# Attention beside a gated feed-forward gate: down-projection transposed, six output row buffers, a reciprocal placed later, and ScalarE in the end stage

## The chip, the core and the metric

The kernel runs on one core of one Trainium2 chip. A core has TensorE (PE in the profile; PEld is its weight load), VectorE (DVE), ScalarE (ACT), GpSimd (POOL) and SyncE (SP), which here issues nearly all the DMAs. The metric is the device time of one execution in microseconds.

## What is computed

x is 2048 tokens x 640 features, in bf16. The result is x + s * g.

```
xn  = layernorm(x)
qkv = xn @ wqkv                      # 32 heads of 20
s   = (softmax(q k^T / sqrt(20)) v) @ wo
h   = sigmoid(xn @ w_gate) * (xn @ w_up)      # 1728 wide
g   = silu(h @ w_down)
out = x + s * g
```

## The kernel before

Tokens are cut into four chunks of 512 (`QC`), and the heads into eight groups of four (`GH`). A group and a chunk make a block, so there are 32 blocks (`NBLK`), numbered in the order in which they are worked. A block has 64 score tiles: 128 keys by 512 queries of one head.

**The start** normalizes x and writes it transposed to `xnT` (features on the partitions). **The main stage** is one loop from L1240 on. It is a planner that runs when the program is built: it advances a clock `now` in steps of 0.02 us, keeps the time at which each engine is free and each PSUM bank is released, and issues the next instruction of each engine when its own durations (`T_F`, `T_MM`, ...) say that it can run. What it fixes is the order of the instructions on each engine; the waits are semaphores.

The work that it interleaves:

- Score tiles (`score_mm`, L899) and their exponentials. A tile goes to ScalarE (`exp_act`: `pt` for two tiles in the two-bank tiles `scA`, `px` for one in a flexible bank) or to VectorE (`iv`, L1336, then three passes over four tiles, L1030 to L1036, giving `pb`). Whichever engine is free takes the next tile.
- The products with v (`pv_emit`, L937) into one bank, `oacc`.
- The items: k, q and v projections, the gate and up products (`mk_gu`, L665), the down-projection (`mk_down`, L720) and the output projection (`mk_out`, L774). An item takes one of three flexible PSUM banks (`bank`), runs its matmuls in steps between the others' work, and then its ScalarE and VectorE operations; the last of these frees the bank. Matmuls of items are cut in four groups of 32 columns that run side by side (`cols`, L472).

Constants steer the choices: `LEAD` is how far the feed-forward items may run ahead of their due work, `M_ORD` the order of banks tried for an item, `DORD` the order for a score tile of VectorE and `XORD` that for the extra tile of ScalarE.

**Gate.** sigmoid is built from tanh. For each chunk 14 tiles `hT` (features of h on the partitions, 512 tokens) are made. `mk_down` then takes, for each of four token tiles of 128 and two halves of 320 output features, hT as the stationary operand and `wd` as the moving one: 14 steps of four matmuls over 320 columns. Tanh on ScalarE (`td`) and one VectorE pass give the gate with tokens on the partitions, in fp32 (`gqs`). For chunks 0 to 2 it is stored in DRAM (`gq_dram`, L743); for the last chunk it stays in two SBUF buffers (`gq_last`, L714).

**Normalization of a block.** After the last product, `norm_a` (L967) copies `oacc` to `on` on VectorE, and SP sends the row sums to DRAM (`ld`, L972) and back spread over 128 partitions (`lt`, L974). `norm_b` (L977) takes the reciprocal on VectorE (`rt`), sends it out (`rd`, L982) and loads it broadcast (`rl`, four DMAs, L985). GpSimd multiplies (`on_bf`), and `norm_c` moves the result to `oU` by DMAs. The planner puts `norm_b` a fixed time behind the copy: 9.0 us (`T_LT`) for blocks up to 27, and 4.5 us (`T_L2`) for blocks 28 to 30 (L1288).

**Output.** For chunks 0 to 2, `mk_out` projects a token tile in two halves of 320 features, once its block is normalized. `load_out` (L765) brings x and the gate of a tile into one of three buffers in the dead `xnT`, one tile ahead, with no tile loaded ahead across a chunk's end. VectorE multiplies with the gate (L796), GpSimd or, from tile 8 on (`DVE_ADD`), VectorE adds x, and SP stores.

**The end stage** (`chain`, L1135) follows the last product of block 31: copy, transposes and division, then the last part of the output projection into four banks of 512 features (`mains`) and two of the narrow rest (`rest`). VectorE multiplies each wide bank with the gate (`t_main`) and the narrow ones (`t_rest`); GpSimd adds x for the first two tiles, VectorE for the last two; SP and ScalarE's queue store two tiles each (`t_out`).

SP works its queue in order: a DMA that waits holds back all that stand behind it.

Of the kernel before, what the change touches and what calls it, by code (L numbers as in the profile page):

```python
# [52 lines left out]
def kernel(  # L53
# [40 lines left out]

    gq_dram = dram.tile([S, D], FP32, name="gq_dram", tag="gqd", bufs=1)
    NU = (HEADS - PG * GH) // UH
# [350 lines left out]
    T_IV, T_ON = 0.605, 0.60  # L447
    LATE, T_LT, T_OU, T_L2, T_RL = 1.0, 9.0, 1.5, 4.5, 5.6
    T_PASS = (0.1333, 0.1333, 0.27)
# [19 lines left out]
    def mark(*e):  # L469
        return lambda t: ev_at.__setitem__(e, t)  # L470
# [194 lines left out]
    def mk_gu(c, kf, at):  # L665
# [20 lines left out]
        def th():  # L686
            st["t"] = w2.tile([P, QC], BF16, tag="tnh", bufs=2, name="tnh")
            act_imm(st["t"][0:fs, :], st["g"][0:fs, :], ACT.Tanh, 0.5)
# [8 lines left out]
        def th2():  # L697
            st["t"] = w2.tile([P, QC], BF16, tag="tnh", bufs=2, name="tnh")
            act_imm(st["t"][fs:P, :], st["g"][0:fs, :], ACT.Tanh, 0.5)
# [13 lines left out]

    def gq_last(t4):  # L714
        if len(gq_l) == t4 // 2:
            w = w2.tile([P, 2, KD, 2 * P], BF16, tag="wgu", bufs=2, name="gql")
            gq_l.append(w.rearrange("p i k f -> p (i k f)").bitcast(FP32))
        return gq_l[t4 // 2][:, t4 % 2 * D:(t4 % 2 + 1) * D]

    def mk_down(c, t4, h, at):  # L720
        st = {}
        tt = 4 * c + t4

        def alloc():
            st["ps"] = misc_ps()

        def mm(kf):
            cols(st["ps"][:, 0:HD], hT[:, kf, t4 * P:(t4 + 1) * P], wd[:, kf, h * HD:(h + 1) * HD],
                 kf == 0, kf == NFT - 1)

        def th():
            st["td"] = w2.tile([P, HD], BF16, tag="td", bufs=2, name="td")
            act_imm(st["td"], st["ps"][:, 0:HD], ACT.Tanh, 0.25)

        def ev():
            if c == NQC - 1:
                return nc.vector.scalar_tensor_tensor(out=gq_last(t4)[:, h * HD:(h + 1) * HD], in0=st["td"], scalar=1.0,
                                                      in1=st["ps"][:, 0:HD], op0=ALU.add, op1=ALU.mult)
# [6 lines left out]
        return Item([("PE", alloc, [(0.14, lambda kf=kf: mm(kf)) for kf in range(NFT)]),  # L745
                     ("ACT", 0.32, th), ("DVE", 0.40, ev, "free", mark("d", c, t4, h))], at, pre=[("h", c, kf) for kf in range(NFT)])

# [8 lines left out]
    def div_scale(tps, n):  # L756
# [6 lines left out]
        return onq  # L763

    def load_out(tt):  # L765
# [4 lines left out]
        out_tiles[tt] = (o2[:, 0:D], o2[:, D:3 * D].bitcast(FP32))  # L770
        nc.sync.dma_start(out=out_tiles[tt][0], in_=x2[tt * P:(tt + 1) * P, :])
        nc.sync.dma_start(out=out_tiles[tt][1], in_=gq_dram[tt * P:(tt + 1) * P, :])

    def mk_out(tt, h, at):  # L774
        st = {}

        def alloc():
            if h == 0:
                load_out(tt)
                if (tt + 1) % 4:  # L780
                    load_out(tt + 1)
            st["ps"] = misc_ps()
# [5 lines left out]
        def ev():  # L788
            xr, gqr = out_tiles[tt]
            sl = slice(h * HD, (h + 1) * HD)  # L790
            while sum(x[1] == "o" for x in pool_q) > 2:
                x = next(x for x in pool_q if x[1] == "o")
                pool_q.remove(x)
                x[2]()
            tmp = w2.tile([P, 2 * HD], BF16, tag="gqs", bufs=3, name="otmp")[:, 0:HD]
            ins = nc.vector.scalar_tensor_tensor(out=tmp, in0=st["ps"][:, 0:HD], scalar=0.25,  # L796
                                                 in1=gqr[:, sl], op0=ALU.mult, op1=ALU.mult)

            if tt >= DVE_ADD:
                st["tmp"] = tmp  # L800
                return ins

            def part(i):
                cs = slice(h * HD + i * HD // 2, h * HD + (i + 1) * HD // 2)
                add = nc.gpsimd.tensor_tensor(out=xr[:, cs], in0=tmp[:, i * HD // 2:(i + 1) * HD // 2], in1=xr[:, cs], op=ALU.add)
                if h == 1 and i == 1:
                    nc.sync.dma_start(out=out2[tt * P:(tt + 1) * P, :], in_=xr)
                return add
            for i in range(2):
                pool_q.append((now + 0.6, "o", lambda i=i: part(i)))  # L810
            return ins
        def add():
            xr = out_tiles[tt][0][:, h * HD:(h + 1) * HD]
            ins = nc.vector.tensor_tensor(out=xr, in0=st["tmp"], in1=xr, op=ALU.add)
            if h == 1:
# [3 lines left out]
                     ("DVE", 0.40, ev, "free", mark("o", tt, h))] + ([("DVE", 0.24, add)] if tt >= DVE_ADD else []), at, need=ALT + 1 + 2 * (tt // 4),  # L819
                    pre=[("d", tt // 4, t4, i) for t4 in range(4) for i in range(2)] + [("h", 2, kf) for kf in range(NFT)] + (  # L820
                        [("o", tt - 2, 1)] if h == 0 and tt > 1 else []))
# [3 lines left out]
    for c in range(NQC):  # L825
        for kf in range(NFT):
            glu.append(lambda at, c=c, kf=kf: mk_gu(c, kf, at))
        for h in range(2):
            for t4 in range(4):
                glu.append(lambda at, c=c, t4=t4, h=h: [mk_down(c, t4, h, at)])  # L830
    for t in range(4 * NVP):
# [272 lines left out]
    xg = xl.rearrange("p (t u) -> p t u", u=D)  # L1104

    def t_main(t4):
        nc.vector.scalar_tensor_tensor(out=tmps[t4], in0=mains[t4], scalar=0.25, in1=gq_last(t4)[:, 0:512],
                                       op0=ALU.mult, op1=ALU.mult)
        if t4 < 2:
            nc.gpsimd.tensor_tensor(out=tail[t4][:, 0:512], in0=tmps[t4], in1=tail[t4][:, 0:512], op=ALU.add)  # L1110

    def t_rest(i):
        nc.vector.scalar_tensor_tensor(out=tmp[:, 2 * i:2 * i + 2, :],
                                       in0=rest[i][:, 0:2 * EX].rearrange("p (t e) -> p t e", e=EX),
                                       scalar=0.25, in1=gq_l[i].rearrange("p (t u) -> p t u", u=D)[:, :, 512:D],
                                       op0=ALU.mult, op1=ALU.mult)
        (nc.vector if i else nc.gpsimd).tensor_tensor(out=xg[:, 2 * i:2 * i + 2, 512:D], in0=tmp[:, 2 * i:2 * i + 2, :],
                                                      in1=xg[:, 2 * i:2 * i + 2, 512:D], op=ALU.add)

    def t_last(t4):  # L1120
        nc.vector.tensor_tensor(out=tail[t4][:, 0:512], in0=tmps[t4], in1=tail[t4][:, 0:512], op=ALU.add)

# [4 lines left out]

    def t_done(i):
        t_rest(i)
        for t4 in (2 * i, 2 * i + 1):  # L1130
            if i:
                t_last(t4)
            t_out(t4)
# [7 lines left out]
             ("DVE", 0.63, lambda: t_main(0), (10,)), ("DVE", 0.63, lambda: t_main(1), (10,)),  # L1141
             ("DVE", 0.7, lambda: t_done(0), (10,)),
             ("PE", 1.1, lambda: e_late(1), (9,), (0, 1, 2, 3)),
             ("DVE", 0.63, lambda: t_main(2), (14,)), ("DVE", 0.63, lambda: t_main(3), (14,)),
             ("DVE", 1.3, lambda: t_done(1), (14,))]
    chain_end = {}

# [21 lines left out]
    with tc.manual_schedule(engines={ENG.PE, ENG.Activation, ENG.DVE, ENG.Pool}):  # L1169
# [70 lines left out]
        while len(chain_end) < len(chain) or fill or items or glu_items or any(it.i < len(it.ops) for it in active):  # L1240
# [37 lines left out]
            for eng in ("ACT", "DVE"):  # L1278
# [260 lines left out]
```

## Time and profile before

| | us |
|---|---|
| median of 3 runs | 802.56 (802.39 to 802.84) |
| the profiled execution | 803.29 |
| its span | 801.6 |
| PE busy | 779.8 (97%) |
| ScalarE busy | 781.8 (98%) |
| VectorE busy | 770.1 (96%) |
| GpSimd busy | 96.4 (12%) |
| down-projection matmuls, 1792 of 320 columns | 87.0 busy |
| tanh of the down-projection, 32 | 19.8 busy |
| VectorE pass of the down-projection, 24 + 8 | 11.6 + 3.8 busy |
| mean clock of TensorE | 0.999 |

The profile is one execution. Busy time of a group is the union of its instructions, and neighbouring instructions of one engine overlap in the records, so the distance between two starts says more of a price than a duration. `SPq` rows are the issues of DMAs by SP: their duration is that of the issue, and the landing shows only in who waits for it. In brackets behind an instruction stands the idle time of its engine just before it and what ended it. The start stage runs to about 18 us, and the end stage begins at about 790.

### The profile page before, as it was taken

The numbers are of one execution on the slowest core, as the hardware profiler recorded it, in microseconds if no ns is written. First come the engines' busy times: TensorE is split into PE (matmuls) and PEld (weight loads), VectorE is DVE, ScalarE is ACT, GpSimd is POOL, SyncE is SP. The second block draws the span as 40 slices with busy tenths as digits, with TensorE's granted clock in tenths as the row PEclk, the third lists the DMA queues.
The fourth block names the chain that finished last, engine by engine and source line by source line (L and its number), as shares of the span: only waits on it lengthen the run. The fifth ranks groups of instructions, "written<-read, shape, count | busy, mean of one in ns | idle before, by whom it ended". The sixth has DMA issues, their size and how long they took to land.

```text
span 801.6 us, 25384 instructions
## 1 busy us (share of the span) xinstructions
PE 779.8 (97%) x10465; PEld 284.4 (35%) x10465; DVE 770.1 (96%) x1246; ACT 781.8 (98%) x992; POOL 96.4 (12%) x203
## 2 busy tenths in 40 slices
PE   8899999999999999999999999999999999999997
PEld 5523333333433323334332332333333233333332
DVE  7798999999999999989999999999999999999997
ACT  8799999999999999999999999999999999999994
POOL 7200000000000000000000000000000100502302
PEclk9999999999999999999999999999999999999999
DMA  5441212223122223222113232222311332331421
GB/s 162 132 131 49 69 40 73 66 67 81 47 62 67 73 72 100 53 60 65 53 46 89 58 87 73 73 81 62 98 36 61 91 89 53 102 107 23 141 70 55
DMA packets 91851, 60.47 MB, mean 75 GB/s; under 512 B 34891, under 2 KB 85627, under 8 KB 91735
## 3 DMA queue, kind: packets, MB, share of 16 engines
q1 hardware_dynamic: 91447, 58.52, 26.1%
q8 instruction: 82, 1.34, 0.7%
q14 instruction: 34, 0.28, 0.1%
q10 hardware_dynamic: 288, 0.33, 0.1%
HBM read 45.18 MB, written 11.09 MB: 70 GB/s over the span
## 4 chain that ended last, share of the span: by engine, by line
PE 45%; ACT 41%; DVE 7%; issue 5%; DMA 1%; SPq 0%; POOL 0%; DVEq 0%; ACTq 0%; POOLq 0%
ACT pt L83 33%; PE bk L474 18%; PE scA L900 14%; PE oacc L937 9%; ACT px L83 4%; DVE iv L1336 2%; ACT tnh L83 2%; DVE pb L1036 1%; ACT td L83 1%; PE bk L900 1%; DVE pb L1033 1%; PE tp L293 1%; DVE pb L1030 0%; DMA lt<-ld 0%; DMA ld<-on 0%
## 5 line engine op out<-in xcount | busy, mean ns | idle before, releaser
L83 ACT ACTIVATE pt<-scA 128x1024 bf16<-128x1024 f32 (+1 forms) x709 | 708.7, 1188 | 0.7 <-PE bk L900 0.3
L1336 DVE TENSOR_SCALAR iv<-bk 128x512 int16<-128x512 f32 x499 | 332.2, 683 | 12.1 <-PE bk L900 9.6
L900 PE MATMUL scA<-q,kT 32*128 32x512 bf16 x1412 | 275.8, 382 | 8.8 <-ACT pt L83 3.3
L900 PE MATMUL bk<-q,kT 32*128 32x512 bf16 x636 | 207.3, 383 | 0.2 <-DVE iv L1336 0.2
L900 PEld LDWEIGHTS <-kT 32*128 32x128 bf16 x2048 | 88.4, 91 | 262.4 <-issue 251.1
L937 PE MATMUL oacc<-pt,v 128*21 128x512 bf16 x1412 | 178.5, 381 | 0.7 <-ACT pt L83 0.7
L937 PE MATMUL oacc<-pb,v 128*21 128x512 bf16 x998 | 160.8, 382 | 0.0
L474 PE MATMUL bk<-xnT,wgu 128*32 128x512 bf16 x2160 | 157.3, 383 | 0.5 <-DVE iv L1336 0.2
L1036 DVE TENSOR_TENSOR pb<-iv,pb 128x2048 bf16<-128x2048 bf16 (+1 forms) x125 | 151.8, 1214 | 0.7
L990 POOL TENSOR_TENSOR on_bf<-on,rl 128x128 bf16<-128x128 f32 x116 | 54.3, 472 | 626.8 <-DVE iv L1336 189.1
L83 ACT ACTIVATE px<-bk 128x512 bf16<-128x512 f32 x137 | 102.1, 762 | 1.7 <-POOL hT L1178 1.6
L474 PE MATMUL bk<-wd,hT 128*32 128x320 bf16 x1792 | 87.0, 302 | 0.1
L1030 DVE TENSOR_SCALAR pb<-iv 128x2048 int16<-128x2048 int16 (+1 forms) x125 | 86.0, 688 | 0.4
L1033 DVE TENSOR_SCALAR pb<-iv 128x2048 int16<-128x2048 int16 (+1 forms) x125 | 85.9, 688 | 0.0
L937 PEld LDWEIGHTS <-v 128*21 128x21 bf16 x2547 | 53.6, 91 | 76.2 <-issue 53.6
L474 PEld LDWEIGHTS <-wgu 128*32 128x32 bf16 x2160 | 44.5, 95 | 64.3 <-issue 46.3
L474 PEld LDWEIGHTS <-hT 128*32 128x32 bf16 x1792 | 37.5, 95 | 38.2 <-issue 32.7
L474 PE MATMUL bk<-xnT,wu 128*32 128x512 bf16 x640 | 48.5, 383 | 0.6 <-DVE iv L1336 0.2
L937 PE MATMUL oacc<-px,v 128*21 128x512 bf16 x137 | 47.0, 381 | 0.0
L83 ACT ACTIVATE tnh<-bk 128x512 bf16<-128x512 f32 (+1 forms) x56 | 43.4, 776 | 0.1
L691 DVE SCALAR_TENSOR_TENSOR hT<-tnh,bk 128x512 bf16<-128x512 bf16 x52 | 35.4, 680 | 1.0 <-PE bk L900 0.3
L655 PE MATMUL bk<-wv,xnT 128*128 128x160 bf16 x280 | 29.4, 235 | 0.6 <-ACT px L83 0.6
(120 smaller groups left out, 406.2 us busy)
## 6 DMA issues: line engine op xcount, KB each, us to landing
rl<-rd SPq DMA_DIRECT2D x124, 64.0 KB
wgu<-in_B_w_gate_dram SPq DMA_DIRECT2D x24, 320.0 KB
wgu<-in_B_w_up_dram SPq DMA_DIRECT2D x24, 320.0 KB
gq_dram<-gqs SPq DMA_DIRECT2D x24, 160.0 KB
xnT<-gq_dram SPq DMA_DIRECT2D x12, 320.0 KB
xt<-in_A_x_dram SPq DMA_DIRECT2D x16, 160.0 KB
xnT<-in_A_x_dram SPq DMA_DIRECT2D x16, 160.0 KB
out_dram<-xnT SPq DMA_DIRECT2D x14, 160.0 KB
```

The costliest lines, as they stand in the source:

```text
L83: return nc.scalar.add_instruction(mybir.InstActivation(func=func, name=nc.get_next_instruction_name(), engine=ENG.Activation, ins=[nc.sca ...
L293: nc.tensor.transpose(out=tps[k][:, kd, :], in_=xns[k][:, kd * P:(kd + 1) * P], identity=ident)
L474: nc.tensor.matmul(out[j:j + 32, :], lhsT=lhsT[:, j:j + 32], rhs=rhs, start=start, stop=stop, tile_position=(0, j), skip_group_check=True)
L655: nc.tensor.matmul(st["ps"][:, i * 2 * GC:(i + 1) * 2 * GC], lhsT=xn_tok(tts[i], kd), rhs=wvs[pr][:, kd, :], start=(kd == 0), stop=(kd == ...
L691: return nc.vector.scalar_tensor_tensor(out=hT[0:fs, kf, :], in0=st["t"][0:fs, :], scalar=1.0, in1=st["u"][0:fs, :], op0=ALU.add, op1=ALU. ...
L900: nc.tensor.matmul(dst, lhsT=kTs[gc_of(b)[0] % 2][32 * j:32 * j + 32, kt * P:(kt + 1) * P], rhs=qts[b % 3][32 * j:32 * j + 32, :], start=T ...
L937: nc.tensor.matmul(oacc[32 * j:32 * j + DH + 1, :], lhsT=lhsT, rhs=u["src"], start=first, stop=last, tile_position=(0, 32 * j), skip_group ...
L990: ins = nc.gpsimd.tensor_tensor(out=on_bf[:, cs], in0=on[:, cs], in1=rl[:, cs], op=ALU.mult)
L1030: ins = nc.vector.tensor_scalar(out=pb[:, 0, :, :].bitcast(I16), in0=iv, scalar1=0x7F80, scalar2=1, op0=ALU.bitwise_and, op1=ALU.bitwise_or)
L1033: ins = nc.vector.tensor_scalar(out=pb[:, 1, :, :].bitcast(I16), in0=iv, scalar1=0x007F, scalar2=0x3F00, op0=ALU.bitwise_and, op1=ALU.bitw ...
L1036: ins = nc.vector.tensor_tensor(out=pb[:, 1, :, :], in0=iv.bitcast(BF16), in1=pb[:, 1, :, :], op=ALU.mult)
L1336: beat(nc.vector.tensor_scalar(out=d["iv"][:, j, :], in0=bank[bk], scalar1=B_OFF, scalar2=0.0, op0=ALU.add, op1=ALU.max))
```

## The change

- `mk_down` takes `wd` as the stationary operand and `hT` as the moving one: 20 items, one for each chunk and each 128 output features, of 14 steps over 512 token columns. Tanh (`td`, now in the three buffers of `tnh`) and the VectorE pass are over 512 columns. The gate then has features on the partitions, in bf16, in the one buffer `gqs`; a DMA transpose on SP, placed 0.8 us (`T_GT`) behind, brings tokens back onto the partitions (`g4`, one buffer), and for chunks 0 to 2 a store to `gq_dram` (now bf16) is placed 5.8 us (`T_GO`) behind. For the last chunk the transpose writes one buffer, `gq_last`.
- Six output buffers instead of three, each of x and a bf16 gate; `load_out` runs up to four tiles ahead (`AHEAD`), when the tile's gate is done and its buffer's former tile has been projected.
- `norm_b` of block 28 is placed 9.0 us behind the copy, as for the blocks ahead of it; 29 and 30 keep 4.5 us.
- In the end stage ScalarE copies the last wide bank, scaled, to SBUF, and VectorE multiplies that copy; the narrow rest of all four tiles is added in one VectorE instruction, ahead of the four stores.
- `LEAD` 40 to 30, `M_ORD` 1 to 0, `DORD` 2 to 0, `XORD` 0 to 1.

```diff
-URGENT, ROUNDS, HOLD, SLACK, LEAD, LAG, D_LAST, D_LAST_END = 0.2, 6, 0.0, 0.0, 40.0, 2.0, 20, 20
-M_ORD, WAIT3, FALL, M_END = 1, 0.2, 1, 2.0
+URGENT, ROUNDS, HOLD, SLACK, LEAD, LAG, D_LAST, D_LAST_END = 0.2, 6, 0.0, 0.0, 30.0, 2.0, 20, 20
+M_ORD, WAIT3, FALL, M_END = 0, 0.2, 1, 2.0
-XMAX, DQ, DORD, XORD, STARVE = 2, 1.4, 2, 0, 0.3
+AHEAD = 4
+XMAX, DQ, DORD, XORD, STARVE = 2, 1.4, 0, 1, 0.3
...
-    gq_dram = dram.tile([S, D], FP32, name="gq_dram", tag="gqd", bufs=1)
+    gq_dram = dram.tile([S, D], BF16, name="gq_dram", tag="gqd", bufs=1)
...
-    def mk_down(c, t4, h, at):
+    def gq_last():
+        if not gq_l:
+            w = w2.tile([P, 2, KD, 2 * P], BF16, tag="wgu", bufs=2, name="gql")
+            gq_l.append(w.rearrange("p i k f -> p (i k f)")[:, 0:4 * D].rearrange("p (t u) -> p t u", u=D))
+        return gq_l[0]
+
+    def mk_down(c, e, at):
...
-            cols(st["ps"][:, 0:HD], hT[:, kf, t4 * P:(t4 + 1) * P], wd[:, kf, h * HD:(h + 1) * HD],
-                 kf == 0, kf == NFT - 1)
+            cols(st["ps"], wd[:, kf, e * P:(e + 1) * P], hT[:, kf, :], kf == 0, kf == NFT - 1)
...
-            flush("o")
-            gqs = w2.tile([P, HD], FP32, tag="gqs", bufs=3, name="gqs")
-            ins = nc.vector.scalar_tensor_tensor(out=gqs, in0=st["td"], scalar=1.0, in1=st["ps"][:, 0:HD],
+            gqs = w2.tile([P, QC], BF16, tag="gqs", bufs=1, name="gqs")
+            ins = nc.vector.scalar_tensor_tensor(out=gqs, in0=st["td"], scalar=1.0, in1=st["ps"],
                                                  op0=ALU.add, op1=ALU.mult)
-            nc.sync.dma_start(out=gq_dram[tt * P:(tt + 1) * P, h * HD:(h + 1) * HD], in_=gqs)
+            es = slice(e * P, (e + 1) * P)
+            g4 = w2.tile([P, 4, P], BF16, tag="g4", bufs=1, name="g4") if c < NQC - 1 else gq_last()[:, :, es]
+            timed.append((now + T_GT, lambda: nc.sync.dma_start_transpose(out=g4, in_=gqs)))
+            if c < NQC - 1:
+                timed.append((now + T_GO, lambda: nc.sync.dma_start(
+                    out=gq_dram[c * QC:(c + 1) * QC, es].rearrange("(t p) u -> p t u", p=P), in_=g4)))
             return ins
...
-        o2 = xfl[:, tt % 3 * KD * QC:tt % 3 * KD * QC + 3 * D]
+        o2 = xfl[:, tt % 6 * 2 * D:(tt % 6 + 1) * 2 * D]
...
-            if h == 0:
-                load_out(tt)
-                if (tt + 1) % 4:
-                    load_out(tt + 1)
+            load_out(tt)
+            n = len(out_tiles)
+            if n < NOUT and n <= tt + AHEAD and (n < 6 or ("o", n - 6, 1) in ev_at) and all(
+                    ("d", n // 4, i) in ev_at for i in range(KD)):
+                load_out(n)
...
+    def t_copy(t4):
+        act_imm(tmps[t4], mains[t4], ACT.Copy, 0.25)
+
     def t_main(t4):
+        if t4 == 3:
+            nc.vector.tensor_tensor(out=tmps[t4], in0=tmps[t4], in1=gq_last()[:, t4, 0:512], op=ALU.mult)
+            return
...
+    def t_done():
+        nc.vector.tensor_tensor(out=xg[:, :, 512:D], in0=tmp, in1=xg[:, :, 512:D], op=ALU.add)
+        t_out(0)
+        t_out(1)
+        for t4 in (2, 3):
+            t_add(nc.vector, t4)
             t_out(t4)
...
-                    timed.append((free["DVE"] + (T_LT if norm_pending[0] < NBLK - 4 else T_L2), norm_pending[0]) + norm_a(norm_pending[0]))
+                    timed.append((free["DVE"] + (T_LT if norm_pending[0] < NBLK - 3 else T_L2), norm_pending[0]) + norm_a(norm_pending[0]))
```

More of the change, by code (lines that the diff above doesn't have):

```diff
@@ L686, in th @@
         def th():
-            st["t"] = w2.tile([P, QC], BF16, tag="tnh", bufs=2, name="tnh")
+            st["t"] = w2.tile([P, QC], BF16, tag="tnh", bufs=3, name="tnh")
             act_imm(st["t"][0:fs, :], st["g"][0:fs, :], ACT.Tanh, 0.5)
@@ L697, in th2 @@
         def th2():
-            st["t"] = w2.tile([P, QC], BF16, tag="tnh", bufs=2, name="tnh")
+            st["t"] = w2.tile([P, QC], BF16, tag="tnh", bufs=3, name="tnh")
             act_imm(st["t"][fs:P, :], st["g"][0:fs, :], ACT.Tanh, 0.5)
@@ L727, in mm @@
         def mm(kf):
-            cols(st["ps"][:, 0:HD], hT[:, kf, t4 * P:(t4 + 1) * P], wd[:, kf, h * HD:(h + 1) * HD],
-                 kf == 0, kf == NFT - 1)
+            cols(st["ps"], wd[:, kf, e * P:(e + 1) * P], hT[:, kf, :], kf == 0, kf == NFT - 1)
         def th():
-            st["td"] = w2.tile([P, HD], BF16, tag="td", bufs=2, name="td")
-            act_imm(st["td"], st["ps"][:, 0:HD], ACT.Tanh, 0.25)
+            st["td"] = w2.tile([P, QC], BF16, tag="tnh", bufs=3, name="td")
+            act_imm(st["td"], st["ps"], ACT.Tanh, 0.25)
@@ L743, in ev @@
-            nc.sync.dma_start(out=gq_dram[tt * P:(tt + 1) * P, h * HD:(h + 1) * HD], in_=gqs)
-            return ins
-        return Item([("PE", alloc, [(0.14, lambda kf=kf: mm(kf)) for kf in range(NFT)]),
-                     ("ACT", 0.32, th), ("DVE", 0.40, ev, "free", mark("d", c, t4, h))], at, pre=[("h", c, kf) for kf in range(NFT)])
+            gqs = w2.tile([P, QC], BF16, tag="gqs", bufs=1, name="gqs")
+            ins = nc.vector.scalar_tensor_tensor(out=gqs, in0=st["td"], scalar=1.0, in1=st["ps"],
+                                                 op0=ALU.add, op1=ALU.mult)
@@ new lines, in ev @@
+            es = slice(e * P, (e + 1) * P)
[4 more added lines that the diff above has]
+                    out=gq_dram[c * QC:(c + 1) * QC, es].rearrange("(t p) u -> p t u", p=P), in_=g4)))
+            return ins
+        return Item([("PE", alloc, [(T_MM, lambda kf=kf: mm(kf)) for kf in range(NFT)]),
+                     ("ACT", 0.48, th), ("DVE", 0.60, ev, "free", mark("d", c, e))], at, pre=[("h", c, kf) for kf in range(NFT)])
@@ L763, in div_scale @@
         return onq
+    NOUT = 4 * (NQC - 1)
     def load_out(tt):
@@ L794, in ev @@
                 x[2]()
-            tmp = w2.tile([P, 2 * HD], BF16, tag="gqs", bufs=3, name="otmp")[:, 0:HD]
+            tmp = w2.tile([P, HD], BF16, tag="ot", bufs=3, name="otmp")
             ins = nc.vector.scalar_tensor_tensor(out=tmp, in0=st["ps"][:, 0:HD], scalar=0.25,
@@ L819, in mk_out @@
                      ("DVE", 0.40, ev, "free", mark("o", tt, h))] + ([("DVE", 0.24, add)] if tt >= DVE_ADD else []), at, need=ALT + 1 + 2 * (tt // 4),
-                    pre=[("d", tt // 4, t4, i) for t4 in range(4) for i in range(2)] + [("h", 2, kf) for kf in range(NFT)] + (
+                    pre=[("d", tt // 4, i) for i in range(KD)] + [("h", 2, kf) for kf in range(NFT)] + (
                         [("o", tt - 2, 1)] if h == 0 and tt > 1 else []))
@@ L827 @@
             glu.append(lambda at, c=c, kf=kf: mk_gu(c, kf, at))
-        for h in range(2):
-            for t4 in range(4):
-                glu.append(lambda at, c=c, t4=t4, h=h: [mk_down(c, t4, h, at)])
+        for e in range(KD):
+            glu.append(lambda at, c=c, e=e: [mk_down(c, e, at)])
     for t in range(4 * NVP):
@@ L1104, with t_add @@
     xg = xl.rearrange("p (t u) -> p t u", u=D)
+    def t_add(eng, t4):
+        eng.tensor_tensor(out=tail[t4][:, 0:512], in0=tmps[t4], in1=tail[t4][:, 0:512], op=ALU.add)
+    def t_copy(t4):
+        act_imm(tmps[t4], mains[t4], ACT.Copy, 0.25)
     def t_main(t4):
-        nc.vector.scalar_tensor_tensor(out=tmps[t4], in0=mains[t4], scalar=0.25, in1=gq_last(t4)[:, 0:512],
+        if t4 == 3:
+            nc.vector.tensor_tensor(out=tmps[t4], in0=tmps[t4], in1=gq_last()[:, t4, 0:512], op=ALU.mult)
+            return
+        nc.vector.scalar_tensor_tensor(out=tmps[t4], in0=mains[t4], scalar=0.25, in1=gq_last()[:, t4, 0:512],
                                        op0=ALU.mult, op1=ALU.mult)
         if t4 < 2:
-            nc.gpsimd.tensor_tensor(out=tail[t4][:, 0:512], in0=tmps[t4], in1=tail[t4][:, 0:512], op=ALU.add)
+            t_add(nc.gpsimd, t4)
     def t_rest(i):
@@ L1114, in t_rest @@
                                        in0=rest[i][:, 0:2 * EX].rearrange("p (t e) -> p t e", e=EX),
-                                       scalar=0.25, in1=gq_l[i].rearrange("p (t u) -> p t u", u=D)[:, :, 512:D],
+                                       scalar=0.25, in1=gq_last()[:, 2 * i:2 * i + 2, 512:D],
                                        op0=ALU.mult, op1=ALU.mult)
[L1117 to L1121, printed above, removed]
     def t_out(t4):
@@ L1141 @@
              ("DVE", 0.63, lambda: t_main(0), (10,)), ("DVE", 0.63, lambda: t_main(1), (10,)),
-             ("DVE", 0.7, lambda: t_done(0), (10,)),
+             ("DVE", 0.40, lambda: t_rest(0), (10,)),
              ("PE", 1.1, lambda: e_late(1), (9,), (0, 1, 2, 3)),
-             ("DVE", 0.63, lambda: t_main(2), (14,)), ("DVE", 0.63, lambda: t_main(3), (14,)),
-             ("DVE", 1.3, lambda: t_done(1), (14,))]
+             ("ACT", 0.55, lambda: t_copy(3), (14,)),
+             ("DVE", 0.63, lambda: t_main(2), (14,)), ("DVE", 0.40, lambda: t_rest(1), (14,)),
+             ("DVE", 0.35, lambda: t_main(3), (15,)), ("DVE", 1.05, lambda: t_done(), (14,))]
     chain_end = {}
```

17 lines of the change are left out of this document (2 added, 15 removed).

## The prediction

> **What bounds the kernel now.** I began with the page's busy totals, went to the chain that ended last, then to the costliest groups with the idle time in front of them, then to the list of waits, and last to the lists of instructions in order of time for the down-projection and for the end.
>
> ```profile
> PE 779.8 (97%) x10465; PEld 284.4 (35%) x10465; DVE 770.1 (96%) x1246; ACT 781.8 (98%) x992; POOL 96.4 (12%) x203
> PE 45%; ACT 41%; DVE 7%; issue 5%; DMA 1%; SPq 0%; POOL 0%; DVEq 0%; ACTq 0%; POOLq 0%
> 200.00:300.00 100.00, 99.03 (x1438) 34.51 (x1432) 98.38 (x158) 100.00 (x129) 9.08 (x20) 1.00 0.23 64
> ```
>
> Three engines are full together. Between 200 and 300 us ScalarE has no gap at all, VectorE is 98% busy, and the chain changes hands between PE and ScalarE. The reason is that the exponentials are shared: a score tile goes either to ScalarE or to VectorE. From the rows below, ScalarE needs some 0.93/2 = 0.465 us per tile; VectorE needs 0.60 for the first step and (0.60 + 0.60 + 1.13)/4 = 0.58 for its part of the three passes, 1.18 in all. Together they do 2.15 + 0.85 = 3.0 tiles per us, so a us freed on ScalarE is worth 0.72 us of span, one on VectorE 0.28, if the written order of the work spreads it; PE I weigh with its share of the chain, 0.45.
>
> ```profile
> 209.08 0.60 ACT L83 ACTIVATE td<-bk 128x320 bf16<-128x320 f32 x1
> 209.40 0.78 ACT L83 ACTIVATE px<-bk 128x512 bf16<-128x512 f32 x1
> 209.87 1.22 ACT L83 ACTIVATE pt<-scA 128x1024 bf16<-128x1024 f32 x1
> ...
> 736.05 0.69 DVE L1336 TENSOR_SCALAR iv<-bk 128x512 int16<-128x512 f32 x1
> 736.65 0.48 DVE L737 SCALAR_TENSOR_TENSOR gql<-td,bk 128x320 f32<-128x320 bf16 x1
> 737.04 0.69 DVE L1336 TENSOR_SCALAR iv<-bk 128x512 int16<-128x512 f32 x1
> ...
> 755.39 0.59 PE L474 MATMUL bk<-wd,hT 128*32 128x320 bf16 x12
> 759.67 1.00 PE L474 MATMUL bk<-wd,hT 128*32 128x320 bf16 x24
> ...
> 450.79 0.61 PE L474 MATMUL bk<-xnT,wgu 128*32 128x512 bf16 x8
> 459.71 1.26 PE L474 MATMUL bk<-xnT,wgu 128*32 128x512 bf16 x20
> ```
>
> Columns are start, duration, engine, line. Neighbours overlap, so the price of an instruction is the distance between starts: a ScalarE pass over 320 columns 0.32 us, over 512 columns 0.47; a VectorE pass from PSUM 0.39 to 0.41 against 0.60. Four column matmuls run side by side: 320 columns take (1.00 - 0.59)/3 = 0.137 us per four, 512 columns (1.26 - 0.61)/3 = 0.217.
>
> ```profile
> 726.36 0.53 SPq L972 DMA_DIRECT2D ld<-on  x1
> 728.06 0.35 SPq L974 DMA_DIRECT2D lt<-ld  x1
> ...
> 746.60 2.61 SPq L771 DMA_DIRECT2D xnT<-in_A_x_dram  x2
> 749.30 0.56 SPq L972 DMA_DIRECT2D ld<-on  x1
> ...
> 729.62 0.25 DVE L980 RECIPROCAL rt<-lt 128x16 f32<-128x16 f32 x1 [0.79 <-DMA lt<-ld]
> 753.64 0.25 DVE L980 RECIPROCAL rt<-lt 128x16 f32<-128x16 f32 x1 [0.66 <-DMA lt<-ld]
> ```
>
> These are the only VectorE waits for a DMA after the start stage. The row sums of blocks 28 and 29 come back too late for a reciprocal placed 4.5 us behind the copy. For block 29 the SP queue shows why: two loads into output tiles stood in front of `ld` until 749.2, although the copy had ended at 747.7.
>
> **The change, part by part.** The profiled execution took 803.29 us (span 801.6 and 1.7 around it), 0.73 above the median of 802.56 that I predict against.
>
> Transposed down-projection. PE: 32 items x 14 x 0.137 = 61.4 us become 20 x 14 x 0.217 = 60.8, 0.6 less; at 0.45 that is -0.3 (0 if ScalarE stays the limit, -0.6 at most). ScalarE: 32 x 0.32 = 10.2 become 20 x 0.47 = 9.4 to 9.6, 0.7 less, -0.5. VectorE: 32 x 0.40 = 12.8 become 20 x 0.60 = 12.0, 0.8 less, -0.2. Reading the gate as bf16 instead of fp32 in the output stage I cost at nothing: the other operand is in PSUM, and that pass takes 0.48 for 320 columns with an fp32 gate at L796, just as L737 with a bf16 operand does.
>
> The 20 DMA transposes are new and no row shows one. Issued 0.8 us behind the VectorE pass, with the store to DRAM 5.0 us later, they replace 24 stores by 20 transposes and 15 stores, all on SP's queue; `gqs` and `g4` have one buffer each. Queued behind a late transpose or a store that waits for it are `ld`, `lt`, `rd`, `rl`, the loads of q and wgu and the oU moves; the next item's VectorE pass waits for `gqs`, and behind that pass stand all VectorE exponentials. The lower bound is the store's 0.35 us of issue plus a landing as of `lt` (728.06 to 729.62, 1.6 in all); the upper one four separate moves, as of `oU<-on_bf x4` with 3.04 us of issue, plus 1.6, near 5. Room: gqs passes come 5.2 us apart (209.84, 214.69, 220.00, 225.18), and 1.5 times as wide that is 7.8. Less 0.8, and less 3.1 of SP queue as in the first chunk (gqs ended at 204.95, stored at 208.05), 3.9 us remain. For the row sums at 203.88, `ld` went out at 207.43 and `lt` at 209.36, so it landed near 210.9, and the reciprocal ran at 213.91: 3.0 us of room. I take a transpose as one move of 128 KB, nearer to the single store than to four moves, which fits both rooms with a few misses: +0.4 (0 to +6, the second worked out below).
>
> Six output buffers, filled up to four tiles ahead. SP no longer waits for an output store before it may reuse one of three buffers (7.8 us in five waits at L771), and block 29's `ld` can leave at 747.7. The 0.66 us wait then goes, unless a transpose now stands there: -0.3 (0 to -0.7). The loads hide behind matmuls, as VectorE's output passes show no idle time; without that cover one costs its landing, 1.6.
>
> Block 28's reciprocal at 9.0 instead of 4.5. The 0.79 us wait goes, on the chain, which passes through `ld` and `lt` there: -0.8 (0 if the transposes eat the room). Moved 4.5 us later with it: the `rd` issue, four `rl` issues, four GpSimd products of 0.47 and the oU moves of block 28. The output tiles of that chunk ask for block 29, which is 23 us behind, so nobody is late next. On GpSimd's queue only the output adds stand behind, and they had idle time.
>
> End stage. Today VectorE runs from 795.42: two wide passes, one narrow (796.63), the strip add (797.08) and two adds until 798.34. With the last bank copied by ScalarE, idle since 793.7, VectorE does one wide pass (0.60), one narrow (0.39), one SBUF product (0.34 by the adds at 797.59), a strip add over all four tiles (0.34) and two adds (0.68), done near 797.8. GpSimd's adds run until 796.9, and beside them a strip add took 0.59, so part of the 0.6 is lost: -0.4 (-0.1 to -0.6). The stores follow the same 2.9 us behind.
>
> Bank order, lead and fewer items (20 instead of 32 hold a PSUM bank until ScalarE and VectorE are through). Nothing in the trace prices a new order. Its gain is bounded by VectorE's 9.6 us of waiting for scores, x 0.28 = -2.7; a loss I bound at the same size. Fewer holders free banks, so I take -0.5.
>
> The sum is -0.3 - 0.5 - 0.2 + 0.4 - 0.3 - 0.8 - 0.4 - 0.5 = -2.6: 800.7 in the profiled execution's terms, 800.0 against the median. A difference under 0.2% (1.6 us) can't be told from none.
>
> **The rivals.** First, slower: the transpose holds SP's queue and `gqs` too long. It decides from about 4 us per transpose on, where both rooms end. At 5.2 us, 20 items x 7.8 = 156 us of the 774 us hold some 6 of the 31 reciprocals, each 2.2 late, 13 us; a third of the 20 passes find `gqs` 1.3 us late, 9 us. 22 us of VectorE x 0.28 = +6, and 800.0 - 0.4 + 6 = 805.6. For it: one buffer each, and an SP queue that is already seen 3.1 us late. Against it: VectorE's room at 9.0 us, and a down-projection in only a fifth of the span. The Trainium skill, page "VectorE: DVE Perf Modes", section "The three transpose paths", gives 1309 ns for a 128x128 block through the DMA; four of them are an estimate of 5.2 us, and by it this rival would hold. The Trainium skill, page "Advanced Engine Details and Errata", section "X-Bar Transpose (TRN2)", says that such DMAs are as fast as regular ones, which would be the lower bound. No run here shows either. Chance 0.24.
>
> Second, hidden: PE's and the end's shares are swallowed because ScalarE has no gap, and a transpose takes the places of both removed waits. Left are -0.5 - 0.2 - 0.1 = -0.8: 801.8. For it speaks the unbroken ScalarE; against it that the removed waits lie on the chain. Chance 0.16.
>
> Third, the bank order pays in full: -2.7 instead of -0.5, 797.8 or lower. For it: 16 waits of VectorE for scores, up to 1.5 us; against it: they are 1% of its time. Chance 0.12.
>
> **How the numbers follow.** The forecast's own case has 0.48. Faster is that and the third rival, 0.60; within 0.2% the second, 0.16; slower the first, 0.24. The range goes from 796.5, the third rival with the best ends of stalls and end stage, to 805.6, the first rival; some 0.05 and 0.12 lie outside. The likeliest case alone spans 798.5 to 800.9.
>
> **What would show it.** Right: 20 `td` rows at 512 columns with 0.47 to 0.48 between starts, no `rt` wait for `lt<-ld` on the block that had 0.79, no L771 wait for `out_dram`, the last VectorE add before 798.0 at an equal start of the end stage. Wrong: idle time in front of `gqs` that a DMA ends, `rt` rows with several waits, SP rows of several us at the transposes, or fewer ScalarE exponentials in the down-projection. If the reciprocals wait again, the first rival is true; if VectorE's waits for scores grow past 10 us, the order lost.

## The result and the profile after

The changed kernel takes 806.12 us (805.1 to 806.72) against 802.70 for the kernel before in the same comparison: ratio 1.0043, 95% interval 1.0033 to 1.0053. It is 3.4 us slower, where 2.6 us faster was forecast, and 0.5 us above the range.

The page of the changed kernel: busy totals, and the chain that ended last.

```profile
PE 774.1 (96%) x9792; PEld 264.1 (33%) x9792; DVE 767.6 (96%) x1233; ACT 782.4 (97%) x984; POOL 96.3 (12%) x202
ACT 55%; PE 23%; DVE 12%; issue 8%; DMA 1%; SPq 0%; POOL 0%; DVEq 0%; ACTq 0%; POOLq 0%
```

TensorE's busy time fell by 5.7 us and VectorE's by 2.5, so their work did shrink. ScalarE's rose by 0.6, although its tanh passes of the down-projection fell from 19.8 to 14.4. The span grew, from 801.6 to 803.4: the time went into waits. (The profiled execution took 805.1 us, the fastest of the changed kernel, and that of before 803.29, one of its slower ones, so the two profiles show 1.8 us of the 3.4.) Where it goes is seen from the start of VectorE's copy of `oacc` at the end of each of the last blocks:

| copy of block | 28 | 29 | 30 | 31 | span |
|---|---|---|---|---|---|
| before | 723.38 | 746.98 | 770.07 | 790.91 | 801.6 |
| after | 723.58 | 744.43 | 771.43 | 792.69 | 803.4 |

At block 27's copy the changed kernel is 0.8 us behind (703.95 against 703.12), at 28's 0.2, and at 29's it leads by 2.5. From 29 to 30 it takes 27.0 us instead of 23.1. These are that stretch's rows of SP's queue, VectorE and ScalarE, in the changed kernel:

```profile
744.43 0.68 DVE L972 COPY on<-oacc 128x512 f32<-128x512 f32 x1
...
743.34 0.38 SPq L810 DMA_DIRECT2D out_dram<-xnT  x1
745.66 0.33 SPq L773 DMA_DIRECT2D xnT<-in_A_x_dram  x1
746.08 3.05 SPq L1022 DMA_DIRECT2D oU<-on_bf  x4
749.23 0.53 SPq L974 DMA_DIRECT2D ld<-on  x1
749.86 0.39 SPq L810 DMA_DIRECT2D out_dram<-xnT  x1
751.72 0.33 SPq L976 DMA_DIRECT2D lt<-ld  x1
...
753.35 0.25 DVE L982 RECIPROCAL rt<-lt 128x16 f32<-128x16 f32 x1 [3.52 <-DMA lt<-ld]
...
757.08 1.02 ACT L84 ACTIVATE pt<-scA 128x1024 bf16<-128x1024 f32 x1 [2.55 <-PE scA L902]
...
760.60 1.94 ACT L84 ACTIVATE pt<-scA 128x1024 bf16<-128x1024 f32 x2 [0.97 <-PE bk L902]
```

Block 29's copy ends at 745.1, but `ld`, its row sums, leaves only at 749.23: a load, held from about 743.7 until 745.66, and then the four `oU` moves of block 28 stand in front. The reciprocal, placed 4.5 us behind the copy, holds VectorE for 3.52 us. TensorE then waits for a bank that VectorE has not read, 2.25 us until 755.39, and ScalarE, too, runs dry, for 2.55 and 0.97 us. The 0.79 us wait of block 28 is gone, and a wait more than four times as long stands at block 29.

The end stage of the changed kernel, on VectorE, ScalarE and GpSimd:

```profile
792.69 0.42 DVE L1070 COPY on<-oacc 128x256 f32<-128x256 f32 x1 [4.76 <-PE oacc L939]
...
796.42 0.60 ACT L84 ACTIVATE hT<-scA 128x512 bf16<-128x512 f32 x1 [0.83 <-PE scA L1063]
796.57 2.25 POOL L1109 TENSOR_TENSOR xnT<-hT,xnT 128x512 bf16<-128x512 bf16 x2 [12.70 <-DVE hT L1118]
...
797.99 1.12 DVE L1116 TENSOR_TENSOR hT<-hT,gql 128x512 bf16<-128x512 bf16 x1
...
799.36 0.74 DVE L1109 TENSOR_TENSOR xnT<-hT,xnT 128x512 bf16<-128x512 bf16 x2
```

From the first copy to the last add it takes 7.41 us; in the profile of before it was 790.91 to 798.34, 7.43. VectorE had also stood idle for 4.76 us ahead of it, against 1.43 before.

### The profile page after: what moved, and what is told of

Same layout as the page of the kernel before. It is cut to its first block, busy times and chain, and to the rows that moved or that the text cites. A ratio compares the mean times of both kernels' runs of the same rounds, so it can differ in the third digit from the quotient of the medians.

```text
span 803.4 us, 24011 instructions
## 1 busy us (share of the span) xinstructions
PE 774.1 (96%) x9792; PEld 264.1 (33%) x9792; DVE 767.6 (96%) x1233; ACT 782.4 (97%) x984; POOL 96.3 (12%) x202
## 4 chain that ended last, share of the span: by engine, by line
ACT 55%; PE 23%; DVE 12%; issue 8%; DMA 1%; SPq 0%; POOL 0%; DVEq 0%; ACTq 0%; POOLq 0%
ACT pt L84 43%; PE bk L475 9%; PE scA L902 7%; ACT px L84 6%; PE oacc L939 5%; DVE iv L1344 5%; ACT tnh L84 3%; DVE pb L1038 2%; DVE pb L1032 1%; DVE pb L1035 1%; ACT td L84 1%; DVE hT L692 1%; ACT aq L175 0%; ACT sq L272 0%; DMA xt<-in_A_x_dram 0%
## 5 line engine op out<-in xcount | busy, mean ns | idle before, releaser
L84 ACT ACTIVATE pt<-scA 128x1024 bf16<-128x1024 f32 x708 | 698.8, 1165 | 3.8 <-PE scA L902 2.5
L902 PE MATMUL bk<-q,kT 32*128 32x512 bf16 x639 | 203.3, 384 | 2.5 <-DVE iv L1344 2.3
L939 PE MATMUL oacc<-pt,v 128*21 128x512 bf16 x1409 | 185.2, 382 | 1.4 <-ACT pt L84 1.4
L902 PEld LDWEIGHTS <-kT 32*128 32x128 bf16 x2048 | 86.1, 91 | 289.0 <-issue 278.7
L939 PE MATMUL oacc<-pb,v 128*21 128x512 bf16 x996 | 162.5, 383 | 0.0
L475 PE MATMUL bk<-xnT,wgu 128*32 128x512 bf16 x2160 | 159.1, 383 | 0.8
L475 PE MATMUL bk<-hT,wd 128*32 128x512 bf16 x1120 | 83.0, 385 | 0.5 <-DVE hT L703 0.2
L84 ACT ACTIVATE tnh<-bk 128x512 bf16<-128x512 f32 (+1 forms) x56 | 41.5, 741 | 0.1
L475 PEld LDWEIGHTS <-wd 128*32 128x32 bf16 x1120 | 20.7, 95 | 36.2 <-issue 29.5
```

What stands on the lines that cost most here:

```text
L84: return nc.scalar.add_instruction(mybir.InstActivation(func=func, name=nc.get_next_instruction_name(), engine=ENG.Activation, ins=[nc.sca ...
L475: nc.tensor.matmul(out[j:j + 32, :], lhsT=lhsT[:, j:j + 32], rhs=rhs, start=start, stop=stop, tile_position=(0, j), skip_group_check=True)
L902: nc.tensor.matmul(dst, lhsT=kTs[gc_of(b)[0] % 2][32 * j:32 * j + 32, kt * P:(kt + 1) * P], rhs=qts[b % 3][32 * j:32 * j + 32, :], start=T ...
L939: nc.tensor.matmul(oacc[32 * j:32 * j + DH + 1, :], lhsT=lhsT, rhs=u["src"], start=first, stop=last, tile_position=(0, 32 * j), skip_group ...
```

## The experiments

"Theory P" is the placement of the reciprocals on SP's queue, "O" the new bank order, "T" the transposes. The medians of the kernel before lie between 802.7 and 803.3 in all comparisons. Edits are shown shortened to the places that differ, and `...` marks what is left out of them and of the views.

**Block 28's reciprocal early again** (changed kernel).

```diff
-(T_LT if norm_pending[0] < NBLK - 3 else T_L2)
+(T_LT if norm_pending[0] < NBLK - 4 else T_L2)
```

> The changed kernel with one part undone: block 28's reciprocal again 4.5 us behind its copy. Theory P (placement): the reciprocal placed later sends block 28's four oU moves down SP's queue just ahead of the row sums of block 29, VectorE waits 3.52 us for them, and that is most of the loss: the wait for lt on block 29 falls to 1 us or less, and the time to 803.0 to 804.0. Theory O (order): the new bank order and lead cost the time, and theory T (transposes): SP's queue is held by the transposes; by both the time stays between 805.3 and 806.6, whatever becomes of that wait.

804.88 us, 1.0026 of before (1.0017 to 1.0035): 1.2 us better, less than P asked for and more than O and T allowed. Block 29's wait went, as P said, but a long one came back at block 28. SP's queue and VectorE of this kernel:

```profile
725.50 0.76 SPq L1022 DMA_DIRECT2D oU<-on_bf  x1
726.37 1.23 SPq L740 DMA_TRANSPOSE gql<-gqs  x1
727.65 0.75 SPq L1022 DMA_DIRECT2D oU<-on_bf  x1
728.51 0.53 SPq L974 DMA_DIRECT2D ld<-on  x1
729.09 1.50 SPq L1022 DMA_DIRECT2D oU<-on_bf  x2
730.70 0.42 SPq L976 DMA_DIRECT2D lt<-ld  x1
...
732.40 0.25 DVE L982 RECIPROCAL rt<-lt 128x16 f32<-128x16 f32 x1 [2.71 <-DMA lt<-ld]
```

Now a transpose, which holds SP for 1.23 us, and the moves of block 27 stand ahead of `ld` and `lt`. So this run does not part P from T: both fill the same queue. The long stretch moved with the wait: from copy 28 to copy 29 it takes 24.84 us (changed kernel: 20.85), from 29 to 30 22.29 (27.00).

**The old bank order** (changed kernel).

```diff
-LEAD 30.0 ... M_ORD 0 ... DORD 0, XORD 1
+LEAD 40.0 ... M_ORD 1 ... DORD 2, XORD 0
```

> The changed kernel with the four constants of the old order (LEAD 40, M_ORD 1, DORD 2, XORD 0). Theory O: 803.5 or less. Theories P and T: 805 to 807, with a wait of several us for lt on block 29 still there by P, or several smaller ones near transposes by T. As every instruction after the start is ordered anew, the waits of VectorE and ScalarE have to be read as well as the time.

807.26 us, 1.0050 (1.0037 to 1.0063). Not faster: in the changed kernel the new constants cost nothing, and whether they gain cannot be told, as the interval overlaps the changed kernel's (1.0033 to 1.0053). The wait for `lt` on block 29 is 4.29 us here. O falls as the cause of the loss.

**The new bank order alone** (kernel before).

```diff
-LEAD 40.0 ... M_ORD 1 ... DORD 2, XORD 0
+LEAD 30.0 ... M_ORD 0 ... DORD 0, XORD 1
```

> The kernel before with only the four constants changed (LEAD 30, M_ORD 0, DORD 0, XORD 1). Theory O: 805 to 806.5, most of the loss without the rest of the change. Theories P and T: within 1 us of 802.6.

810.97 us, 1.0100 (1.0087 to 1.0113), more than any theory said. Its list of VectorE's waits:

```profile
DVE iv L1336 <- PE bk L900: 14.5, 31, 1.1
DVE rt L980 <- DMA lt<-ld: 7.3, 5, 3.5
```

Waits for scores grew from 9.6 to 14.5 us, and those for row sums from 1.5 to 7.3. The same constants cost the kernel before 8 us and the changed kernel nothing: they are not a part with a price of its own.

**VectorE reads the last wide bank** (changed kernel).

```diff
-        if t4 == 3:
-            nc.vector.tensor_tensor(out=tmps[t4], in0=tmps[t4], in1=gq_last()[:, t4, 0:512], op=ALU.mult)
-            return
...
-("ACT", 0.55, lambda: t_copy(3), (14,)),
-("DVE", 0.63, lambda: t_main(2), (14,)), ("DVE", 0.40, lambda: t_rest(1), (14,)),
-("DVE", 0.35, lambda: t_main(3), (15,)),
+("DVE", 0.63, lambda: t_main(2), (14,)), ("DVE", 0.63, lambda: t_main(3), (14,)),
+("DVE", 0.40, lambda: t_rest(1), (14,)),
```

> The changed kernel with VectorE again reading the last wide bank from PSUM (no ScalarE copy), all else as changed. The prediction's step of -0.4 for the end stage says 806.5. The rival from the trace says that the gain is lost: the product of the copied bank took 1.12 us beside GpSimd's add, where 0.34 was counted, so without it the end stage is as long, 806.1 within 0.3, and the last add ends 7.2 to 7.6 us behind the copy of oacc.

806.07 us, 1.0038 (1.0026 to 1.0050): no change in time. Its end stage:

```profile
793.98 0.42 DVE L1070 COPY on<-oacc 128x256 f32<-128x256 f32 x1 [4.76 <-PE oacc L939]
...
798.28 1.28 DVE L1115 SCALAR_TENSOR_TENSOR hT<-scA,gql 128x512 bf16<-128x512 f32 x2
...
800.34 0.75 DVE L1109 TENSOR_TENSOR xnT<-hT,xnT 128x512 bf16<-128x512 bf16 x2
```

793.98 to 801.09 is 7.11 us, a little under what was expected and 0.3 shorter than with ScalarE's copy.

**Blocks 28 and 29 both late** (changed kernel): the run that tests the placement itself.

```diff
-(T_LT if norm_pending[0] < NBLK - 3 else T_L2)
+(T_LT if norm_pending[0] < NBLK - 2 else T_L2)
```

> The changed kernel with the reciprocal of block 29, too, 9.0 us behind its copy (block 30 keeps 4.5). Theory P, that VectorE's wait for late row sums costs the time: no wait of VectorE for lt over 0.5 us, ScalarE's 2.5 and 1.0 us waits near 757 and 760 gone, 802.5 to 804.0. Rival N, that the wait is slack which VectorE would have spent elsewhere (it stands 4.8 us idle at the last block anyway): 805.3 or more. Second rival: with the reciprocal later, the oU moves of block 29 come late for the output tiles of that chunk, and a wait of PE or VectorE near 770 to 780 takes its place.

801.70 us, 0.9986 of before (0.9977 to 0.9995), 4.4 us under the changed kernel. SP's queue, the reciprocal of block 29 and VectorE's next copy:

```profile
745.95 3.05 SPq L1022 DMA_DIRECT2D oU<-on_bf  x4
749.10 0.53 SPq L974 DMA_DIRECT2D ld<-on  x1
...
751.66 0.33 SPq L976 DMA_DIRECT2D lt<-ld  x1
...
753.98 0.24 DVE L982 RECIPROCAL rt<-lt 128x16 f32<-128x16 f32 x1
...
754.48 0.38 SPq L984 DMA_DIRECT2D rd<-rt  x1
...
766.71 0.68 DVE L972 COPY on<-oacc 128x512 f32<-128x512 f32 x1
```

SP's queue is as crowded as in the changed kernel, and `ld` as late. But the reciprocal now asks later, VectorE has no wait for `lt` on any block, ScalarE's two waits are down to one of 0.56 us, and block 30's copy comes at 766.71 instead of 771.43. So the crowded queue alone did not cost the time; it did so together with a VectorE instruction in order that asked too early. Block 30 keeps 4.5 us and does not wait: the moves of block 29 are through at 763.82, ahead of its copy. Rival N falls; of the second rival nothing is seen. The order of the work behind block 29 is new here too, so that all of the 4.4 us is the wait's is argued: where the wait stands, the stretch to the next copy is 4 to 5 us longer than without it (24.84 against 20.86 behind block 28, 27.00 against 22.30 behind 29).

One more rival lies in the traces: TensorE's granted clock. In the changed kernel it was 1.00 from 752 to 756 us and 0.57 from 756 to 760, shortly behind TensorE's idle time. But with both late it was 0.61 from 760 to 764, and that kernel is fast. The same kernel with another end stage (both late, VectorE reading the last wide bank, below) was profiled at 1.00 there, and from copy 29 to copy 31 it takes 44.45 us against 44.83. So by these two profiles the low clock cost some 0.4 us, and it does not part the versions; its share of the changed kernel's loss was not measured.

**Output tiles two ahead** (changed kernel).

```diff
-AHEAD = 4
+AHEAD = 2
```

> The changed kernel with output tiles loaded two ahead instead of four (AHEAD 2). By the trace the loads four ahead wait on SP for the store of the tile six back, 6.5 us in five waits. If these waits push block 29's row sums, they vanish here, ld of block 29 goes out about 1.6 us sooner behind its copy, the wait for lt falls from 3.5 to about 2, and the time by about 1, to 805. If only the oU moves matter, the wait stays at 3 us or more and the time at 806.

806.18 us, 1.0035 (1.0023 to 1.0048), and the wait for `lt` is 3.41 us. SP still waits 5.8 us in four waits for output stores, and the one ahead of block 29's `ld` is among them. So the edit did not remove what it was to remove; that load's share of the delay was not parted from the `oU` moves'.

**Block 28's reciprocal late, alone** (kernel before).

```diff
-(T_LT if norm_pending[0] < NBLK - 4 else T_L2)
+(T_LT if norm_pending[0] < NBLK - 3 else T_L2)
```

> The kernel before with only block 28's reciprocal moved to 9.0 us. The prediction's step says that the 0.79 us wait goes and nothing else comes late: 802.0. Theory P says that block 28's oU moves reach SP's queue 4.5 us later and stand in front of block 29's row sums: its wait grows from 0.66 to 2 or 3 us, and the time is 803.5 to 805.

805.28 us, 1.0029 (1.0018 to 1.0041). The edit alone costs 2.4 us. SP and VectorE:

```profile
747.36 0.56 SPq L972 DMA_DIRECT2D ld<-on  x1
748.02 3.02 SPq L1020 DMA_DIRECT2D oU<-on_bf  x4
751.14 0.42 SPq L974 DMA_DIRECT2D lt<-ld  x1
...
752.83 0.25 DVE L980 RECIPROCAL rt<-lt 128x16 f32<-128x16 f32 x1 [1.61 <-DMA lt<-ld]
```

Here the four moves of block 28 stand between `ld` and `lt`. VectorE's waits for row sums are 2.1 us in all, 0.6 more than before, so they are not the whole 2.4. In the trace the loss stands later: at block 30's copy (769.85) this kernel is still 0.2 us ahead of the kernel before, at block 31's (792.41) it is 1.5 behind, and its end stage takes 8.47 us instead of 7.43. In between the last gate pass slid from 770.67 to 790.03, where VectorE waited 1.46 us for its tanh. So the wait grew at block 29 as P said, but that it cost the 2.4 us here is not shown.

**The down-projection transposed, alone** (kernel before, with three bf16 output buffers).

```diff
-cols(st["ps"][:, 0:HD], hT[:, kf, t4 * P:(t4 + 1) * P], wd[:, kf, h * HD:(h + 1) * HD], ...)
+cols(st["ps"], wd[:, kf, e * P:(e + 1) * P], hT[:, kf, :], ...)
...
+timed.append((now + T_GT, lambda: nc.sync.dma_start_transpose(out=g4, in_=gqs)))
```

> The kernel before with only the down-projection transposed (bf16 gate, transposes and stores on SP, three output buffers, old constants, old reciprocals, old end stage). The prediction's steps for it sum to -0.3 - 0.5 - 0.2 + 0.4 = -0.6: 802.3. Theory T, that the transposes hold SP's queue: 804 or more with waits of VectorE for lt at the blocks whose copies lie beside the transposes. A move of the time by several us with no new wait at all would say that the new order of the work, which every part of the change sets off, outweighs the parts.

803.64 us, 1.0015 (1.0006 to 1.0023): 0.7 slower, 1.3 off the step, and less than T asked for. VectorE waits for `lt` once, 1.08 us, no more than before, and never for `gqs` to come free. The profiled execution's span of 801.2 is no longer than that of before, so the trace does not hold the loss, and its place stays open. What the trace does show is a lead of 1.4 us at block 27's copy (701.73), of which 0.5 is left at block 31's (790.38).

**Blocks 28 and 29 both late** (kernel before).

```diff
-(T_LT if norm_pending[0] < NBLK - 4 else T_L2)
+(T_LT if norm_pending[0] < NBLK - 2 else T_L2)
```

> The kernel before with the reciprocals of blocks 28 and 29 both 9.0 us behind their copies, nothing else changed. If the waits for late row sums are all that parts the versions, this gains too: no wait for lt over 0.6 us and 801.0 to 802.0, and then the 1.2 us by which the changed kernel with both placed late beats the kernel before is the reciprocals', not the rest of the change. If the transposed down-projection and the six buffers bring something of their own, this stays at 802.5 or more.

802.37 us, 0.9993 (0.9984 to 1.0002): between the two expectations, no difference that can be measured. With both reciprocals out of harm's way in both kernels, the rest of the change stands at 801.70 against 802.37, which the intervals do not part. VectorE has no wait for `lt` here, and yet the stretch from copy 29 to copy 30 takes 25.33 us, against 25.08 with the 1.61 us wait of the run with block 28 alone: a wait of that size cost its stretch nothing. The last gate pass is back at 770.1. The medians, with the ratios' intervals some 0.8 us to either side:

| reciprocals 9.0 us behind | up to 27 | up to 28 | up to 29 |
|---|---|---|---|
| kernel before | 802.9 | 805.3 | 802.4 |
| changed kernel | 804.9 | 806.1 | 801.7 |

By the medians, stopping at 28, as the change does, is the worst of the three in both.

**VectorE works longer in the last block** (changed kernel, both late).

```diff
-D_LAST_END = 20
+D_LAST_END = 16
```

> The changed kernel with both reciprocals late, and VectorE taking score tiles of the last block until 16 are left instead of 20 (D_LAST_END). There VectorE stood idle 3.6 us in front of the end stage while ScalarE worked off the last tiles. If that imbalance costs, VectorE's wait falls to 2 us or less and the time by 0.3 to 1.0, to 801; if the last block's end is set by TensorE and ScalarE in any case, it stays at 801.7 within 0.4.

801.58 us, 0.9987 (0.9978 to 0.9996). The idle time of VectorE ahead of the end stage fell to 1.85 us, as expected, and the time did not follow: 0.1 us by the medians is no difference. In its end stage VectorE's pass over the bank beside ScalarE's copy waits for that copy, and the product of the copy takes 0.41 us, behind GpSimd's adds:

```profile
792.62 2.26 POOL L1109 TENSOR_TENSOR xnT<-hT,xnT 128x512 bf16<-128x512 bf16 x2 [12.71 <-DVE hT L1118]
793.34 0.60 ACT L84 ACTIVATE hT<-scA 128x512 bf16<-128x512 f32 x1 [1.90 <-PE scA L1063]
...
793.97 0.69 DVE L1118 SCALAR_TENSOR_TENSOR hT<-scA,gql 128x512 bf16<-128x512 f32 x1 [0.85 <-ACT hT L84]
...
794.90 0.41 DVE L1116 TENSOR_TENSOR hT<-hT,gql 128x512 bf16<-128x512 bf16 x1
```

**VectorE reads the last wide bank** (changed kernel, both late): the edit of the fourth run on the fifth.

> The changed kernel with both reciprocals late, and the last wide bank read from PSUM by VectorE instead of copied by ScalarE. In the profile of the same edit on the changed kernel the end stage took 7.1 us from the copy of oacc to the last add, against 7.4 with ScalarE: the copy costs 0.3 instead of gaining 0.4. Expected 801.4, and the stage at 7.0 to 7.2 us; by the prediction's step 802.1 and 7.8.

801.45 us, 0.9987 (0.9978 to 0.9995); the stage takes 788.89 to 796.00, 7.11 us, as expected. The time agrees with 801.4, but 0.25 us against 801.70 is not clear of the noise.

**The three edits together** (changed kernel).

> The changed kernel with the three edits that did not lose: both reciprocals late, VectorE reading the last wide bank, VectorE taking tiles of the last block until 16 are left. If the small gains of the last two add up (0.1 and 0.25 by their medians, the second 0.3 by the profile of the stage), 801.2 to 801.5 and the fastest version so far; if they are noise, 801.7.

800.81 us against 803.27 for the kernel before, 0.9972 (0.9962 to 0.9983): the fastest version by its median, about 2.4 us under the kernel before and 0.4 under what was expected.

## Why the prediction was wrong

**The step that failed is "Block 28's reciprocal at 9.0 instead of 4.5", priced at -0.8.** Alone it costs the kernel before 2.4 us, and undoing it in the changed kernel gives back 1.2. The 0.79 us wait did go, as said. But the step listed what moves with the reciprocal, four `oU` moves among it, and then asked only who needs block 28's result: "so nobody is late next". It did not ask whose DMAs stand behind the moved ones on SP's queue. Those were block 29's row sums, still asked for after 4.5 us: the wait there grew from 0.66 to 3.52 us, with a load held by an output store ahead of the moves. The run with both late shows the place: SP's rows up to `lt` stay as they were, the wait goes, and 4.4 us come back. For the changed kernel this is shown. In the kernel before the wait grew too, but the 2.4 us stand behind block 30, in a new order of the work, and their cause is open.

**"Six output buffers", -0.3, was wrong.** SP's waits for output stores went from 7.8 us to 6.5, still five. The loads run ahead until they meet the buffer of a tile that is multiplied but not yet stored (store at 743.34, load held until 745.66). And block 29's wait did not go but grew. What the buffers are worth by themselves was not measured.

**"Transposed down-projection" and its transposes, -0.6 in all, measured +0.7 alone.** The prices per pass were right (`td` 0.47 between starts at 713.10, gate pass 0.59 at 205.39). Why the whole did not gain is open.

**"End stage", -0.4, rested on the copy, and the copy costs the stage 0.3** (7.41 against 7.11 in the changed kernel, 7.43 against 7.11 with both late), though no difference in time could be measured. The step saw that GpSimd's adds would be beside it and took only part of the gain off; in fact the product, counted at 0.34, took 1.12 us and ended 0.29 behind GpSimd (below). The whole stage, 7.41 against 7.43, has no clean price: in the four other traces with the old stage it took 8.12 to 8.47, as TensorE still had eight instead of four matmuls of the output projection to run ahead of the last two wide banks.

**"Bank order", -0.5 within 2.7 either way:** as a bound on what an order can cost it was far too narrow. The same constants moved the kernel before by +8; in the changed kernel the -1.1 by the medians is not clear of the noise.

**The first rival** came true in sign and nearly in time (805.6 against 806.1), not in its mechanism; that the times are so near is luck. Row sums that come late on SP's queue were its place. But no pass waited for `gqs`, and at block 29 no transpose stood in the queue: they issue in 1.2 us, and one landed within 2.45 (below), under its point of 4. The holders there were a load that waited for a store and the `oU` moves at 0.75 us each, and both kinds were there before. The second (801.8) and the third (797.8) did not come; VectorE's waits for scores, which the third does away with, went only from 9.6 us to 9.1.

The measured time is 6.1 us from the forecast (806.1 against 800.0). Of these, 4.4 went when both reciprocals were late. The other 1.7 is as much as the end stage (0.4) and the down-projection (1.3) missed their terms by, but as the bank order shows, the parts do not add here, so that this is the split is not shown.

## What to carry to other kernels

When a step is moved later, follow each DMA that it issues down its queue and ask who stands behind it there, not only who needs its result. A fixed delay in an in-order engine is a bet on the queue that feeds it: when one delay is moved, move those with it whose DMAs then come to stand behind. And where every edit sets off a new order of the work, price an edit by undoing it in the changed kernel, since a constant that costs one order nothing can cost another several us.

## What was not expected

A DMA transpose of 128x512 bf16 holds SP for 1.2 us, where a store of 128 KB holds it for 0.38. Rows of the transposes in the changed kernel, with min, median and max in ns, then one, with the store behind it that waits for its landing:

```profile
L740 SPq DMA_TRANSPOSE g<-gqs x15: 1202/1231/2410, 210.8 to 602.5; - x15
L742 SPq DMA_DIRECT2D gq_dram<-g x15: 365/383/451, 213.4 to 608.4; - x15
...
592.59 1.20 SPq L740 DMA_TRANSPOSE g<-gqs  x1
593.89 0.52 SPq L984 DMA_DIRECT2D rd<-rt  x1
595.04 0.37 SPq L742 DMA_DIRECT2D gq_dram<-g  x1
```

It landed within 2.45 us, issue included. The estimate of 5.2 us, worked out from the block time in the Trainium skill, page "VectorE: DVE Perf Modes", section "The three transpose paths", does not hold here; the sentence of the Trainium skill, page "Advanced Engine Details and Errata", section "X-Bar Transpose (TRN2)", that such DMAs are as fast as regular ones, is nearer.

VectorE's product of two SBUF tensors took 1.12, 0.68 and 0.41 us in three kernels with the same end stage: the changed one, both late, and both late with VectorE working longer. It began 0.83 and 0.41 us before GpSimd's adds ended (798.82 and 795.39), and in the third just after (794.88): each time it ended 0.27 to 0.43 us behind them. By that it does not run beside GpSimd but waits; VectorE's pass over a PSUM bank beside the same adds kept its 0.69 us (797.05). The Trainium skill, page "SBUF — State Buffer", section "SBUF: two separate sides", describes it so: a VectorE operation with two SBUF inputs and a GpSimd operation that reads SBUF take a shared pair of ports in turn, each for its whole length. These rows agree.

VectorE's pass over the other bank of the same two-bank PSUM tile began only when ScalarE's copy had ended (793.97 after 793.94, with 0.85 us of idle time). In the changed kernel, too, it began at 797.05, after a copy that ended at 797.02. Whether the chip or the program's own waits ask for that was not tried.
